# Exponentials on VectorE by the slot of four banks, layer-norm transposes by DMA, and two open sums in place of turn-taking by key chunk

## The chip, the cores and the metric

The kernel runs on one core of one Trainium2 chip. The metric is the device time of one execution in microseconds (us), the median of three runs. Engine names follow the profile: PE is the matrix engine (PEld its weight loads), DVE is VectorE, ACT is ScalarE, POOL is GpSimd, and SP is the engine whose queue (SPq) issues the DMAs.

## The reference, cut to what matters

One transformer layer over S = 2048 tokens of width D = 640, batch 1. The attention has 32 heads of 20 channels and no mask. The second half is a bilinear gate with 1728 hidden channels.

```python
x = A_x
h = x + attention(layernorm(x), A_wqkv, A_wo)       # softmax(q k^T / sqrt(20)) v, 32 heads
n = layernorm(h)
h2 = h + ((n @ B_w_gate) * (n @ B_w_up)) @ B_w_down
```

Inputs and output are bfloat16. The softmax needs 32 x 2048 x 2048 exponentials, and that is what the kernel is built around.

## The kernel before, in words

**Tiling.** Heads are taken in 8 groups of 4 (`G`, `HP`). The four heads of a group lie in the four 32-row bands of the partitions. Queries are cut into six blocks of 512, 512, 384, 256, 256 and 128 (`WIDTHS`). For a block `p` and a group `g`, scores are made transposed: 128 keys on the partitions, queries along the free side. A *slot* is (p, g, kg): 512 columns of (key tile, query) for each of the four heads, that is four PSUM banks of 128x512. There are 512 slots and 2048 banks. `att.flat` counts banks handed out.

**Exponentials.** PE fills one of two PSUM areas, `A0` of three banks and `A1` of two, with a burst of score matmuls (`s_act`), and ACT turns the area into a bf16 tile `E` with one ACTIVATE (`exp`, L731). The two areas alternate, so ACT instructions are of three banks and of two. About one bank in seven goes to DVE instead (`dexp`, `tail`, L738 to L790). DVE adds a bias and writes int16 (L745), and after every second bank it runs four more instructions over the pair (1024 columns: L769, L772, L775, L778), into tiles of their own (`i16`, `fr`, `hl`, `ED`). Such a bank comes from one of two spare PSUM banks `m` or from the third bank of `A0`. `SHARE` = 0.17 caps what DVE takes, counted from `D_START` = 128 banks.

**Sums.** For each slot PE multiplies E with V (`pv_act`) into one PSUM bank `acc`, which holds the four heads' 20 channels and their denominators. A *stretch* is a run of slots whose sum lies in `acc`. For the first block the first two groups take turns: four slots of group 0, four of group 1, then again for the next 512 keys, because the keys of chunk `c` of 512 come into being while the attention already runs. After each of the first three turns DVE copies or adds `acc` into an SBUF tile (`partial`, L873), and at the last turn `normalise` adds the rest (L898). `normalise` then sends the denominators out and back by three DMAs on SP's queue: `rs` (L905), a reciprocal on DVE (L906), `rd` (L907), `rb` (L911), and the product goes to `OnT` (L917).

**Projections.** Stage 1 (`stage1_ln`) makes the layer norm of four token tiles at a time on DVE and POOL. PE transposes each tile (five 128x128 blocks, `transpose_group`, L1009) and DVE or ACT copies the result into `lnT` (L1026, L1024). Keys and queries of groups 0 and 1 are projected straight into place (`proj_direct`). Those of groups 2 to 7 (`proj_dense`) are copied to `stg`, written to DRAM (`kq`, L1208, L1211), and read back spread out (`kT` L1225, `qT` L1222). Twenty small DMAs (L1237, L1243) put zeros into `kq`'s padding; each row that is read back needs them. V is projected in three parts (`proj_v`). The order and the due times of these groups stand at the end of the function (L1482 to L1520): V of a chunk is queued one chunk late, and `LEADK` = 16 brings the keys and queries of later groups forward.

**Second stage.** When a block's attention is done, `second_stage` (L1326) queues the output projection `wo`, the second layer norm (`l2`), its PE transposes into `ln2T` (L1376), the gate and up matmuls (`gs`, `hh`) and the down matmul (`ot`). For all blocks but the last ones this is background work that fills PE between score bursts.

**Order.** The function is a planner that runs while the program is built. It keeps a clock for each engine, and at each step it emits the instruction that its estimates put next (`Engines.run`, `Pe.choose`). What comes out is one fixed order for each engine and for SP's queue, and each engine works through its own strictly. Where the planner expects PE to be idle it puts in multiplications by zero (`fill`, tile `zt`).

Of the kernel before, what the change touches and what calls it, by code (L numbers as in the profile page):

```python
# [44 lines left out]
LASTP = len(WIDTHS) - 1  # L45
RES = 5
FAST_LAST = 2
# [145 lines left out]
class Pe:  # L193
# [91 lines left out]
    def fill(self, s):  # L285
        bank = self.att.summing()
        new = bank is None
        deps = [self.zeros]
        if new:
            b = next((b for b in self.mbanks if b.free.t is not None and b.free.t <= s), None)  # L290
            if b is None:
                b = Bank(self.att.acc)
                b.free = self.att.acc_free
            bank, deps = b.ap, deps + [b.free]
        n = bank.shape[1]
        self.charge(s, n / 2.4 + 3.0, self.shape(), float(n), deps, [])
        self.filler(bank, new)
# [30 lines left out]
NED = 4  # L328
NI16 = 3
# [10 lines left out]
LEADK = 16  # L340
# [4 lines left out]
def kernel(  # L345
# [26 lines left out]
    mb = tiles(psum, 2, [P, QW], F32, "m")  # L372
    pools = [tc.alloc_tile_pool(name="second", bufs=1, space=PSUM)]
    A = [None, pools[0].tile([P, 2, QW], F32, name="A1", tag="A1")]
    A[0] = pools[0].tile([P, 3, QW], F32, name="A0", tag="A0")

    def single_banks():

        if att.flat < att.total or att.a_free[0].t is None or att.a_free[1].t is None or len(pools) > 1:
            return  # L380
        pools[0].release()
# [18 lines left out]
    I16t = tiles(keep, NI16, [P, 2, QW], I16, "i16_")  # L400
    FR = tiles(keep, 2, [P, 2, QW], I16, "fr")
    HL = tiles(keep, 1, [P, 2, QW], BF16, "hl")
    ED = tiles(keep, NED, [P, 2, QW], I16, "ED")
    accS = tiles(keep, 2, [P, QW], F32, "accS")
    rb = tiles(keep, 2, [P, QW], F32, "rb")
    rs = tiles(keep, 6, [P, 16], F32, "rs")
# [64 lines left out]
    class Att:  # L471
        def __init__(self):
# [5 lines left out]
            for p, w in enumerate(WIDTHS):  # L478
                nb = NT * w // QW
                order = [[(g, kg) for kg in range(nb)] for g in range(G)]  # L480
                if p == 0:
                    order = [[(g, 4 * c + i) for i in range(4)] for c in range(NCH) for g in range(2)] + order[2:]
# [10 lines left out]
            self.sums = [len(r) for r in self.stretches]  # L493
# [10 lines left out]
            self.acc = acc[:]  # L504
            self.a_free = [Ev(0.0), Ev(0.0)]
            self.e_use = {0: [[] for _ in EA[0]], 1: [[] for _ in EA[1]], "ED": [[] for _ in ED]}
            self.e_n = {0: 0, 1: 0, "ED": 0}
# [4 lines left out]
            self.acc_free = Ev(0.0)  # L512
            self.dn = 0
            self.pair = []
            self.ipos = 0
            self.i_free = [Ev(0.0) for _ in I16t]
            self.f_free = [Ev(0.0) for _ in FR]
            self.h_free = [Ev(0.0) for _ in HL]
# [61 lines left out]
        def wants_d(self):  # L580
# [4 lines left out]
            if not self.pair and known([self.pv_ev[x] for x in self.e_use["ED"][self.e_n["ED"] % len(ED)]]) == INF:  # L585
                return False
            t = en.free["PE"]
            load = max(0.0, en.free["DVE"] - t) + sum(x.dur for x in en.pend["DVE"] if known(x.deps) < t + 400.0)
            return load < (D_LOAD if self.flat > 2 * HP * NT else D_LOAD0)
# [36 lines left out]
        def summing(self):  # L626

            if self.pv_at >= len(self.stretches):
                return None
            if self.pv_at in self.begun:  # L630
                return acc[:, 0:WIDTHS[self.slots[self.pv_left[0]][0]]]
            return None

        def between(self, t):
# [3 lines left out]
            return self.pv_at not in self.begun and self.acc_free.t is not None and self.acc_free.t <= t  # L638

        def s_option(self, t):  # L640
# [3 lines left out]
            if self.a_free[u].t is None:  # L644
                return INF, None, 0.0
            size = 3 - u
            banks = self.peek(size)
# [5 lines left out]
        def s_act(self, u, banks):  # L653
            def act(s):
                size = len(banks)
                deps = [self.a_free[u]]
# [56 lines left out]
                if self.flush or self.flat == self.total:  # L713
                    self.flush = False
                    if self.pair:
# [22 lines left out]
        def dexp(self, bank, b, ev, readers=None):  # L738
            k = self.ipos % len(I16t)
            pos = len(self.pair)  # L740
            self.taken += 1
            it = I16t[k]
# [4 lines left out]
            e = en.add("DVE", dve_ns(QW), [ev, self.i_free[k]], fn, 0)  # L747
            bank.free = e
            self.pair.append((b, e))
            if len(self.pair) == 2:  # L750
                self.tail()

        def tail(self):
            k = self.ipos % len(I16t)
            self.ipos += 1
            n = len(self.pair)
            N = n * QW
            it = I16t[k]
            fk, hk = self.dn % len(FR), self.dn % len(HL)
            self.dn += 1  # L760
            ek = self.e_n["ED"] % len(ED)
            self.e_n["ED"] += 1
            use = self.e_use["ED"][ek]
            self.e_use["ED"][ek] = sorted({b[0] for b, _ in self.pair})
            f, h, e16 = FR[fk], HL[hk], ED[ek]
            fb = f[:].bitcast(BF16)

            def p2():
                nc.vector.tensor_scalar(f[:, 0:n, :], it[:, 0:n, :], 127, None, ALU.bitwise_and)  # L769

            def p3():
                nc.vector.tensor_scalar(h[:, 0:n, :], f[:, 0:n, :], QR, QK, ALU.subtract, ALU.mult)  # L772

            def p4():
                nc.vector.tensor_tensor(fb[:, 0:n, :], h[:, 0:n, :], f[:, 0:n, :], ALU.mult)  # L775

            def p5():
                nc.vector.tensor_tensor(e16[:, 0:n, :], it[:, 0:n, :], fb[:, 0:n, :], ALU.add)  # L778

            e2 = en.add("DVE", dve_ns(N, 4), [e for _, e in self.pair] + [self.f_free[fk]], p2, 2)  # L780
            e3 = en.add("DVE", dve_ns(N, 4), [e2, self.h_free[hk]], p3, 2)
            e4 = en.add("DVE", dve_ns(N, 2), [e3], p4, 2)
            e5 = en.add("DVE", dve_ns(N, 2), [e4] + [self.pv_ev[s] for s in use], p5, 2)
            self.i_free[k] = e5
            self.f_free[fk] = e5
            self.h_free[hk] = e4
            eb = e16[:].bitcast(BF16)
            for i, (b, _) in enumerate(self.pair):
                self.E[b] = (eb[:, i, :], e5)
            self.pair = []  # L790

        def pv_option(self, t):
# [3 lines left out]
            for s in self.pv_left:  # L796
# [8 lines left out]
                if self.pv_at not in self.begun:  # L805
# [3 lines left out]
                    deps.append(self.acc_free)  # L809
                rt = max(t, known(deps))  # L810
                if rt < best[0]:
                    dur = sum(pe_ns(n) for _, _, n, _ in todo)
                    best = rt, self.pv_act(s, es, todo, deps, dur), dur, "C"
# [4 lines left out]
        def pv_act(self, s, es, todo, deps, dur):  # L818
            p, g, kg = self.slots[s]
            i_s = self.pv_at  # L820

            def act(start):
                pe.charge(start, dur, "C", dur * 2.4, deps, [self.pv_ev[s]])
                self.sums[i_s] -= 1
                first = i_s not in self.begun
                self.begun.add(i_s)
                last = self.sums[i_s] == 0
                for i, (k, q, n, c) in enumerate(todo):

                    opens = first and i == 0  # L830
                    ends = last and i == len(todo) - 1
                    for j in range(HP):
                        h = g * HP + j
                        mm(acc[32 * j:32 * j + 32, q:q + n], Vx[:, k, h * VS:h * VS + 32],
                           es[j][0][:, c:c + n], opens, ends)
# [3 lines left out]
                if last:  # L839
                    if p == 0 and g < 2 and kg < NCH * 3:  # L840
                        self.acc_free = partial(g, kg >= 4, self.pv_ev[s])
                    else:
                        self.acc_free = normalise(p, g, self.pv_ev[s])
# [27 lines left out]
    part_ev = {}  # L871

    def partial(g, more, ev):  # L873

        t = rb[g][:]
        if more:
            part_ev[g] = en.add("DVE", dve_ns(QW), [ev, part_ev[g]], lambda: nc.vector.tensor_tensor(t, acc[:], t, ALU.add), 0.3)
        else:
            part_ev[g] = en.add("DVE", dve_ns(QW), [ev], lambda: nc.vector.tensor_copy(t, acc[:]), 0.3)
        return part_ev[g]  # L880

    FAST = {LASTP: FAST_LAST, LASTP - 1: FAST_PREV}

    def normalise(p, g, ev):
# [11 lines left out]
        if p == 0 and g < 2:  # L896
            free = en.add("DVE", dve_ns(w), [ev, part_ev[g]] + was,
                          lambda: nc.vector.tensor_tensor(a[:, 0:w], acc[:, 0:w], rb[g][:], ALU.add), 0.5)  # L898
        else:
            free = en.add("DVE", dve_ns(w), [ev] + was,  # L900
                          lambda: nc.vector.tensor_copy(a[:, 0:w], acc[:, 0:w]), 0.5)
# [66 lines left out]

    rb_free = [Ev(0.0) for _ in range(8)]
# [60 lines left out]

    def sum_group(deps, mats, n, width, evac, tag):
# [53 lines left out]
    pe.zeros = e_zt  # L1085
    e_id = en.add("POOL", 1500.0, [], lambda: make_identity(nc, ident[:]), 0)
# [16 lines left out]
    def stage1_ln(ch):  # L1103
# [11 lines left out]
        for i in range(TPC):  # L1115
# [8 lines left out]
            def done(r, tt=tt, i=i, ev=ev):  # L1124
                lnT_ev[tt] = r
            g = transpose_group(outs[i], evs[i], lnT[:, :, tt * P:(tt + 1) * P], done,
# [199 lines left out]
    def second_stage(p):  # L1326
# [17 lines left out]
        for tt in range(nt):  # L1344
# [4 lines left out]
            for hf in range(2):  # L1349
# [9 lines left out]
                g = sum_group(T["wo_ev"] + [ex, Later(lambda: on_ev.get((p, G - 1)))], mats, HD, P, evac, f"W{p}{tt}{hf}")  # L1359
# [7 lines left out]
        for a in range(0, nt, step):  # L1367
# [4 lines left out]
            for i, e in zip(idx, evs):  # L1372
                def done(r, i=i):
                    lev[i].t2 = r
                lev[i] = Cell()
                g = transpose_group(l2[i % 2], e, ln2T[:, :, i * P:(i + 1) * P], done, "DVE", 1, f"t{p}{i}")  # L1376
                g.deps.append(fr.get("ln2T") or Ev(0.0))
                fr["ln", i % 2] = g.ev
                groups.append(g)
# [107 lines left out]

    def values(ch):
        for t in range(ch * TPC, (ch + 1) * TPC):
            g = proj_v(t, 0)  # L1490
            g.deps.append(first)
            pe.groups.append(g)

    for ch in range(1, NCH):
# [4 lines left out]
        values(ch - 1)  # L1499
    values(NCH - 1)  # L1500

# [5 lines left out]

    jobs = []
    for T_, when in enumerate((128, 192, 320, 384)):
        jobs.append((when - LEADK, len(jobs), proj_dense(0, T_, 0)))  # L1510
# [55 lines left out]
```

The softmax here doesn't subtract the row's maximum and nothing guards it: scores larger than these inputs give would overflow.

## Time and profile before

| what | us |
|---|---|
| median of 3 runs (lowest, highest) | 875.37 (875.25, 875.66) |
| the profiled execution | 875.66 |
| its span, first to last instruction | 873.6 |
| PE busy / ACT busy / DVE busy / POOL busy | 828.6 / 808.8 / 741.9 / 21.3 |
| first exponential starts | 17.02 |
| last exponential ends | 837.5 |

A busy time is the union of an engine's instructions, so two that overlap are not counted twice. "idle before" is how long the engine had nothing running ahead of an instruction, with the engine and line that ended the wait. A matmul's end is modelled, so a busy PE is not a PE at its peak.

### The profile page before, as it was taken

Reading aid. Unit: us, or ns where it says so; the run is one execution under the profiler, and the core shown is the slowest. Engines: PE = TensorE matmul, PEld = TensorE weight load, DVE = VectorE, ACT = ScalarE, POOL = GpSimd, SP = SyncE. Lnnn points to the kernel's source line nnn. Section 1 sums busy time; section 2 is a strip of 40 time slices with the busy share of each in tenths; the row PEclk is TensorE's granted clock in tenths of the full one; section 3 lists DMA queues with packets and bytes.
Section 4 is the critical chain, followed back from the end, with each engine's and each line's share of the span. In section 5 each row is a group of like instructions: output and inputs, shape, how many; then the busy total and the mean of one; then the engine's idle time right before and its main releaser. Section 6 shows DMA issues by size and latency. Waiting matters only on the chain.

```text
span 873.6 us, 35178 instructions
## 1 busy us (share of the span) xinstructions
PE 828.6 (95%) x15727; PEld 366.7 (42%) x15727; DVE 741.9 (85%) x1579; ACT 808.8 (93%) x771; POOL 21.3 (2%) x33
## 2 busy tenths in 40 slices
PE   6999999989999999999999999999999999999998
PEld 3344333223333322233444333344444444556676
DVE  5654587989879999999989999989999999889562
ACT  4789999999999999999999999999999999998931
POOL 3020000000000000000000000000000000000000
PEclk8899999999999999999999999999999999999999
DMA  7221221222221143320030223134024411164200
GB/s 209 64 58 49 79 67 31 78 76 67 69 79 29 28 105 103 78 63 18 30 91 13 57 66 81 27 84 105 17 51 94 96 32 32 32 150 86 52 6 24
DMA packets 131755, 56.23 MB, mean 64 GB/s; under 512 B 102292, under 2 KB 129556, under 8 KB 131604
## 3 DMA queue, kind: packets, MB, share of 16 engines
q1 hardware_dynamic: 131604, 53.99, 24.3%
q8 instruction: 123, 2.02, 1.0%
q14 instruction: 28, 0.23, 0.1%
HBM read 45.63 MB, written 8.09 MB: 61 GB/s over the span
## 4 chain that ended last, share of the span: by engine, by line
ACT 63%; PE 26%; DVE 6%; issue 5%; DMA 0%; DVEq 0%; POOL 0%; ACTq 0%
ACT E L731 62%; PE m L432 11%; PE A L432 6%; PE acc L432 5%; PE b L432 2%; DVE i L745 2%; DVE fr L775 1%; PE m L1017 1%; DVE ED L778 1%; DVE st L989 0%; DVE fr L769 0%; DVE hl L772 0%; DVE gs L1410 0%; DMA shared<-in_A_x_dram 0%; DVE shared L1001 0%
## 5 line engine op out<-in xcount | busy, mean ns | idle before, releaser
L731 ACT ACTIVATE E<-A 128x1536 bf16<-128x1536 f32 (+1 forms) x749 | 800.0, 1211 | 20.6 <-PE A L432 18.4
L432 PE MATMUL A<-qT,kT 32*128 32x256 bf16 (+3 forms) x3063 | 292.7, 298 | 24.1 <-ACT E L731 21.9
L432 PEld LDWEIGHTS <-kT 32*128 32x128 bf16 (+1 forms) x3448 | 100.1, 92 | 248.2 <-issue 215.0
L432 PE MATMUL acc<-E,Vx 128*32 128x256 bf16 (+3 forms) x2832 | 190.7, 304 | 4.8 <-ACT E L731 3.8
L745 DVE TENSOR_SCALAR i<-m 128x512 int16<-128x512 f32 x176 | 120.4, 685 | 13.5 <-PE m L432 12.5
L432 PEld LDWEIGHTS <-Vx 128*32 128x32 bf16 x3328 | 70.1, 95 | 100.5 <-issue 91.6
L775 DVE TENSOR_TENSOR fr<-hl,fr 128x1024 bf16<-128x1024 bf16 x151 | 103.4, 685 | 2.0
L778 DVE TENSOR_TENSOR ED<-i,fr 128x1024 int16<-128x1024 int16 x151 | 103.0, 682 | 1.3
L745 DVE TENSOR_SCALAR i<-A 128x512 int16<-128x512 f32 x126 | 86.5, 686 | 11.5 <-PE A L432 10.0
L432 PE MATMUL m<-Wd,hh 128*32 128x320 bf16 (+1 forms) x1498 | 79.9, 301 | 1.4 <-issue 0.9
L432 PE MATMUL m<-lnT,Wr 128*32 128x512 bf16 (+7 forms) x1200 | 74.7, 345 | 1.8 <-DVE lnT L1026 0.8
L432 PE MATMUL m<-ln2T,wu 128*32 128x512 bf16 (+2 forms) x980 | 69.5, 348 | 0.8 <-DVE i L745 0.4
L432 PE MATMUL m<-ln2T,wg 128*32 128x512 bf16 (+2 forms) x980 | 69.2, 349 | 0.3 <-DVE hh L1421 0.2
L432 PE MATMUL acc<-zt 128*32 128x512 bf16 (+3 forms) x1012 | 68.5, 346 | 0.0
L432 PE MATMUL m<-qT,kT 32*128 32x256 bf16 (+3 forms) x265 | 68.0, 310 | 0.0
L772 DVE TENSOR_SCALAR hl<-fr 128x1024 bf16<-128x1024 int16 x151 | 63.5, 421 | 1.5
L769 DVE TENSOR_SCALAR fr<-i 128x1024 int16<-128x1024 int16 x151 | 62.1, 417 | 0.7
L432 PEld LDWEIGHTS <-hh 128*32 128x32 bf16 (+2 forms) x1540 | 42.2, 96 | 28.1 <-issue 15.5
L1421 DVE TENSOR_TENSOR hh<-gs,m 128x512 bf16<-128x512 bf16 (+3 forms) x70 | 37.9, 541 | 14.0 <-PE m L432 10.1
L432 PE MATMUL m<-shared,On 128*32 128x320 bf16 x960 | 44.7, 300 | 0.7 <-DVE i L745 0.4
L432 PEld LDWEIGHTS <-Wr 128*32 128x32 bf16 (+1 forms) x1200 | 28.9, 97 | 27.0 <-issue 16.7
L1410 DVE CAST gs<-m 128x512 bf16<-128x512 f32 (+2 forms) x64 | 36.0, 562 | 4.7 <-PE m L432 4.3
(85 smaller groups left out, 542.7 us busy)
## 6 DMA issues: line engine op xcount, KB each, us to landing
wg<-in_B_w_gate_dram SPq DMA_DIRECT2D x47, 160.0 KB
wu<-in_B_w_up_dram SPq DMA_DIRECT2D x47, 160.0 KB
rb<-rd SPq DMA_DIRECT2D x16, 256.0 KB
kT<-kq SPq DMA_DIRECT2D x24, 128.0 KB
kq<-stg SPq DMA_DIRECT2D x24, 120.0 KB
out_dram<-ot SPq DMA_DIRECT2D x16, 160.0 KB
shared<-in_A_x_dram SPq DMA_DIRECT2D x14, 160.0 KB
Wd<-in_B_w_down_dram SPq DMA_DIRECT2D x13, 160.0 KB
```

The source lines that it names most:

```text
L432: nc.tensor.matmul(out_, lhsT=lhsT, rhs=rhs, start=start, stop=stop)
L731: apart(readers, nc.scalar.activation(E[:, 0:size, :], src[:, 0:size, :], ACT.Exp, scale=LN2_ / UNIT))
L745: apart(readers, nc.vector.tensor_scalar(it[:, pos, :], bank.ap, BIAS, 0.0, ALU.add, ALU.max))
L769: nc.vector.tensor_scalar(f[:, 0:n, :], it[:, 0:n, :], 127, None, ALU.bitwise_and)
L772: nc.vector.tensor_scalar(h[:, 0:n, :], f[:, 0:n, :], QR, QK, ALU.subtract, ALU.mult)
L775: nc.vector.tensor_tensor(fb[:, 0:n, :], h[:, 0:n, :], f[:, 0:n, :], ALU.mult)
L778: nc.vector.tensor_tensor(e16[:, 0:n, :], it[:, 0:n, :], fb[:, 0:n, :], ALU.add)
L1017: nc.tensor.transpose(pt[32 * i:32 * i + 32, c * P:(c + 1) * P], src[:, c * P + 32 * i:c * P + 32 * i + 32], ident[:])
L1410: r = en.add("DVE", dve_ns(w), [e, was], lambda: nc.vector.tensor_copy(gs[0:M, 0:w], ps[0:M, 0:w]), 1)
L1421: r = en.add("DVE", dve_ns(w), [e, ce, was], lambda: nc.vector.tensor_tensor(hh[0:M, 0:w], gs[0:M, 0:w], ps[0:M, 0:w], ALU.mult), 1)
```

## The change

Four things change, and since the planner works from estimates, the order on every engine moves with them.

1. **DVE's exponentials.** The pairs become groups of a whole slot. Four banks go to one int16 tile `D` (three such tiles), and the four following instructions then run over 2048 columns at once, the last one in place. `ED`, `i16` and the second `fr` go. `D_START` falls from 128 to 96 and the limit `D_LOAD0` goes.
2. **Transposes.** Those of token chunks 2 and 3 in stage 1, and all of the second stage, become `dma_start_transpose` on SP's queue (`turn_rows`). Chunks 0 and 1 stay on PE.
3. **The first two groups.** Their slots of block 0 form one stretch. Group 1 sums in a second bank `acc2`, so `partial` goes. The bank is taken from `A0`, which has two banks instead of three until both sums are closed.
4. **The order of projections.** V is queued in its own chunk, and V, keys and queries of later groups are queued by simple loops without `LEADK`.

A path `last_quotients` is added for `TURNED` groups; `TURNED` is 0, so nothing of it runs but two small memsets of its tiles `o7`. Its code is left out below, as is bookkeeping of `acc_free` as a pair.

```diff
-NED = 4
-NI16 = 3
+ND = 3
-LEADK = 16
+TURNED = 0
+TURN = 2
-    A[0] = pools[0].tile([P, 3, QW], F32, name="A0", tag="A0")
+    early = tc.alloc_tile_pool(name="early", bufs=1, space=PSUM)
+    A[0] = early.tile([P, 2, QW], F32, name="A0", tag="A0")
+    acc2 = early.tile([P, QW], F32, name="acc2", tag="acc2")
+    late = []
...
-                    order = [[(g, 4 * c + i) for i in range(4)] for c in range(NCH) for g in range(2)] + order[2:]
+                    order = [[(g, 4 * c + i) for c in range(NCH) for g in range(2) for i in range(4)]] + order[2:]
...
+        def acc_of(self, p, g):
+            return acc2[:] if (p, g) == (0, 1) else acc[:]
...
             size = 3 - u
+            if u == 0 and not late and (self.acc_free[1].t is None or self.pv_at == 0 or self.acc_free[1].t > at):
+                size = 2
...
+                if size == 3 and not late:
+                    early.release()
+                    late.append(tc.alloc_tile_pool(name="late", bufs=1, space=PSUM))
+                    A[0] = late[0].tile([P, 3, QW], F32, name="A0", tag="A0")
...
         def dexp(self, bank, b, ev, readers=None):
...
-            e = en.add("DVE", dve_ns(QW), [ev, self.i_free[k]], fn, 0)
+            e = en.add("DVE", dve_ns(QW), [ev] + self.duse, fn, 0)
             bank.free = e
-            self.pair.append((b, e))
-            if len(self.pair) == 2:
-                self.tail()
+            self.group.append((b, e))
 
         def tail(self):
...
+            n = len(self.group)
             N = n * QW
...
-                nc.vector.tensor_tensor(e16[:, 0:n, :], it[:, 0:n, :], fb[:, 0:n, :], ALU.add)
+                nc.vector.tensor_tensor(it[:, 0:n, :], it[:, 0:n, :], fb[:, 0:n, :], ALU.add)
...
-    def partial(g, more, ev):
-
-        t = rb[g][:]
-        if more:
-            part_ev[g] = en.add("DVE", dve_ns(QW), [ev, part_ev[g]], lambda: nc.vector.tensor_tensor(t, acc[:], t, ALU.add), 0.3)
-        else:
-            part_ev[g] = en.add("DVE", dve_ns(QW), [ev], lambda: nc.vector.tensor_copy(t, acc[:]), 0.3)
-        return part_ev[g]
...
+    def turn_rows(src, dst, deps, prio):
+
+        return dma(lambda: nc.sync.dma_start_transpose(dst, src), deps, prio=prio, size=2 * P * D * 2)
...
+            if ch >= TURN:
+                lnT_ev[tt] = turn_rows(outs[i], lnT[:, :, tt * P:(tt + 1) * P], [evs[i]], 0)
+                ln_free[i] = lnT_ev[tt]
+                continue
...
-                lev[i] = Cell()
-                g = transpose_group(l2[i % 2], e, ln2T[:, :, i * P:(i + 1) * P], done, "DVE", 1, f"t{p}{i}")
-                g.deps.append(fr.get("ln2T") or Ev(0.0))
-                fr["ln", i % 2] = g.ev
-                groups.append(g)
+                lev[i] = turn_rows(l2[i % 2][:], ln2T[:, :, i * P:(i + 1) * P], [e, fr.get("ln2T")], 0.5)
+                fr["ln", i % 2] = lev[i]
...
         pe.groups += [proj_direct(1, 0, ch), proj_direct(1, 1, ch)]
-        values(ch - 1)
-    values(NCH - 1)
+        pe.groups += [proj_v(t, 0) for t in range(ch * TPC, (ch + 1) * TPC)]
...
-    jobs = []
+    vq = [(t, 1) for t in range(NT)] + [(t, 2) for t in range(NT)]
     for T_, when in enumerate((128, 192, 320, 384)):
-        jobs.append((when - LEADK, len(jobs), proj_dense(0, T_, 0)))
+        due([proj_dense(0, T_, 0)], when)
         for ch in range(NCH):
-            jobs.append((when + 16 * ch - LEADK, len(jobs), proj_dense(1, T_, ch)))
-    for part, when in ((1, 128), (2, 256)):
-        for t in range(NT):
-            jobs.append((when + 4 * t, len(jobs), proj_v(t, part)))
-    for when, _, g in sorted(jobs, key=lambda x: x[:2]):
-        due([g], when)
+            due([proj_dense(1, T_, ch)], when + 16 * ch)
+            due([proj_v(*vq.pop(0)) for _ in range(4) if vq], when + 16 * ch + 16)
...
-D_START = 2 * HP * NT
+D_START = 96
-D_LOAD0 = 600.0
```

## Prediction

> **What bounds the kernel now.** I read the page's busy times and chain first, then ACT's instructions by shape.
>
> ```profile
> PE 828.6 (95%) x15727; PEld 366.7 (42%) x15727; DVE 741.9 (85%) x1579; ACT 808.8 (93%) x771; POOL 21.3 (2%) x33
> ...
> ACT 63%; PE 26%; DVE 6%; issue 5%; DMA 0%; DVEq 0%; POOL 0%; ACTq 0%
> ```
>
> ```profile
> L731 ACT ACTIVATE E<-A 128x1024 bf16<-128x1024 f32 x501 | 500.2, 1072 | 9.7 <-PE A L432 8.7 <-PE acc L432 0.6
> ...
> L731 ACT ACTIVATE E<-A 128x1536 bf16<-128x1536 f32 x248 | 370.1, 1492 | 10.9 <-PE A L432 9.7 <-ACT E L731 0.4
> ```
>
> ACT carries 63% of the chain that ended last, nearly all in L731. The mean durations overlap, so I price by the median distance from one start to the next: 0.904 us for two banks, 1.330 for three. The 749 take 501 x 0.904 + 248 x 1.330 = 782.7 us of the 820.5 between first start (17.0) and last end (837.5). PE's 95% holds some 77 us of zero filling. The missing 38 us are gaps, the long ones early; ACT's timeline has them in brackets:
>
> ```profile
> 35.04 5.97 ACT L731 ACTIVATE E<-A 128x1536 bf16<-128x1536 f32 x5 [2.86 <-PE A L432]
> ...
> 55.16 29.75 ACT L731 ACTIVATE E<-A 128x1024 bf16<-128x1024 f32 x26 [3.52 <-PE A L432]
> 86.17 27.04 ACT L731 ACTIVATE E<-A 128x1024 bf16<-128x1024 f32 x24 [1.26 <-PE A L432]
> ```
>
> The first two are the waits for chunk 1's and chunk 2's keys; 86.17 is where head group 2 begins. SP's timeline shows how group 2's queries came in time: their read (L1222) goes out before the denominators of groups 0 and 1 (L905).
>
> ```profile
> 32.09 0.48 SPq L1237 DMA_DIRECT2D kq<-zt  x1
> 56.18 1.95 SPq L1269 DMA_DIRECT2D shared<-in_A_wo_dram  x3
> ...
> 76.17 0.44 SPq L1222 DMA_DIRECT2D qT<-kq  x1
> ...
> 79.79 0.60 SPq L905 DMA_DIRECT2D rs<-accS  x1
> ...
> 86.23 0.56 SPq L905 DMA_DIRECT2D rs<-accS  x1
> ```
>
> The hole from 32.6 to 56.2 shows that SP's queue is strict: L1269 waits for POOL, and all stand behind it. At the end PE binds: the last block's transposed norm is ready at 849.7, but PE comes to use it at 857.3.
>
> ```profile
> 848.55 0.45 PE L1014 MATMUL b<-ident,l 128*128 128x128 bf16 x5 [0.32 <-DVE l L1001]
> ...
> 857.27 1.29 PE L432 MATMUL b<-ln2T,qT 128*128 128x128 bf16 x20
> ```
>
> [...] The trace has 0.22 us for a block on PE and no DMA transpose at all.
>
> **The change, part by part.** Counts and order are those of the two built programs, which can be read without running them.
>
> *Exponentials.* DVE takes 317 banks instead of 302. ACT runs 528 twos and 225 threes: 477.3 + 299.3 = 776.6 us, **-6.2 us**. ACT is at its limit, so this is on the path.
>
> *DVE.* Four rows tell the price of a pair.
>
> ```profile
> L775 DVE TENSOR_TENSOR fr<-hl,fr 128x1024 bf16<-128x1024 bf16 x151 | 103.4, 685 | 2.0
> L778 DVE TENSOR_TENSOR ED<-i,fr 128x1024 int16<-128x1024 int16 x151 | 103.0, 682 | 1.3
> ...
> L772 DVE TENSOR_SCALAR hl<-fr 128x1024 bf16<-128x1024 int16 x151 | 63.5, 421 | 1.5
> L769 DVE TENSOR_SCALAR fr<-i 128x1024 int16<-128x1024 int16 x151 | 62.1, 417 | 0.7
> ```
>
> A pair costs 2.21 us, 151 of them 333 us. [...] Fifteen more first passes add 10, 24 copies fewer of transposed blocks save 12, `partial` saves 4: DVE falls by some 35 us. From 280 to 720 us it is busy 424.7 of 440. Yet relief shortens nothing by itself, as ACT ends last there. I take 1 us off later gaps (bounds 0 and 6). Against it, a 1.22 us instruction ahead of a first pass holds a bank up to 0.54 us longer than one of 0.68; the third bank of `A0`, used 120 times, has about 1 us to spare, so I take nothing (bounds 0 and 3).
>
> *PE transposes away, filling added.* 24 tiles leave PE; the fillings rise from 274 to 331 quads. Both lie beside ACT. After the last burst PE has 30.3 us of work by columns instead of 29.9: **+0.5 us**.
>
> *The two open sums.* `A0` has two banks for the first 128 banks: 64 ACT instructions where there were 51. Already in the sum.
>
> *DMA transposes.* A tile is 160 KB. Bounds: 1.8 us from issue to landing (`out<-ot`, the same size, by the trace's semaphore events)[...]. I take about 3 us, overlapping, so chunk 2's four tiles, normalised by about 43.6 (44.8 in this trace, less `partial` and some of chunk 3's statistics queued ahead), lie in `lnT` by 48 to 51. On SP they pass the zero padding and the output-weight loads. DVE's writes of chunk 3's norms wait for them, and V and key copies are queued behind these on DVE. At the very end the transpose may take 8 us before PE misses it.
>
> *Where the order leaves ACT idle.* PE's order between two bursts gives a least gap. I price four matmuls side by side from the lines with many in a row: 0.22 us at 512 columns (36 in 2.13 us), 0.08 at 160 (40 in 0.93), 0.15 at 320 between them.
> - Chunk 1: a run of 2.1 us where there were 3.6; gap 1.0, and 0.4 at a small one later.
> - Chunk 2 (burst 32): after the exponentials that it waits for, PE has queued V, one projection, the keys and 0.9 us of filling: 4.5 us, so a gap of 5.1 with 0.6 for the hand-overs, from about 49 to 54, if the transposes are there by 51.
> - **Group 2 (burst 64).** After the last sum of group 1, which needs the exponentials of burst 63, PE has queued one sum (0.2), three V tiles of 160 (1.2), three projections (3.3), five V tiles of 320 (3.75) and eleven fillings (2.4): 10.1 by columns alone, 10.9 at my prices. SP forces a wait too: the queries' read now stands behind `rd` of group 1, which needs that sum, its copy, `rs` and the reciprocal. That chain is 1.3 us (sum and copy, 84.9 to 86.2 in this trace) + 1.9 (`rs` landing) + 0.3 + issues of 0.4, 0.75 and 0.35 + 3.0 (`qT<-kq` landing) = 8.0. So even without the filling the gap would be about 8. I take 10.8.
> - A run of 2.8 us at burst 103: 1.0.
>
> With the 0.7 at 25.3 as it is, early gaps are 0.7 + 1.0 + 0.4 + 5.1 + 10.8 + 1.0 = 19.0. Before they were 0.69 + 2.86 + 1.05 + 3.52 + 1.26 + 1.17 = 10.6. **+8.4 us.**
>
> **Sum:** -6.2 + 8.4 - 1.0 + 0.5 = +1.7. The profiled execution took 875.7 (span 873.6 and 2.1 around it), 0.3 over the median of 875.4. So 877.1.
>
> **The rivals.**
> - *A, the forecast:* the exponentials saved are given back at group 2's start. 877.1; with the bounds of relief and chunk 2, 874 to 881. Chance 0.5.
> - *B, the transposes by DMA are slow.* Nothing in this trace excludes it. From some 2 us a tile in series, chunk 2's keys come late. At 4 us: 42.6 + 16 + about 2.5 for projection and copy = 61 against 54, +7, and chunk 3, whose norms wait for the same buffers, adds 1.5: 885.6. [...] Chance 0.22.
> - *C, faster: DVE's load was what kept ACT from its rhythm.* The place is 115 to 790 us. Beside the gaps, ACT's small delays (each under 0.3 us beyond the median distance) sum to 16 us in the run, and DVE frees the banks that bursts wait for. If the relief returns 40% of these 16, that is 6 us: 871. It decides from 3.5 us returned. Against it: waits of PE's bursts for DVE are put at 0.6 us in total. Chance 0.28.
>
> **How the numbers follow.** About 0.2% (1.75 us) is what can be told from no change, so 873.6 to 877.1 is "same". Slower holds B and rather more than half of A: 0.53. Same holds the rest of A and a little of C: 0.24. Faster holds the rest of C: 0.23. The range 870.5 to 887.5 takes in C's and B's centres[...]. A's own range stands above.
>
> **What would show it.** Right: ACT idle by 8 to 11 us once, after 64 two-bank exponentials, with `qT<-kq` issued after `rd`; 753 ACT instructions at unchanged distances; PE still last at the end. Wrong: that gap under 4 us (the order says otherwise), a gap well over 5 us before burst 32 (B), or ACT's distances from 115 to 790 nearer the medians (C). DVE's instructions over 2048 columns should show 0.69 and 1.22 us.

## The result and the profile after

The changed kernel takes 890.35 us (median of 4 runs, 888.42 to 891.75), the kernel before in runs beside it 875.31. The ratio is 1.017, 95% interval 1.015 to 1.019: slower by 15 us, above the range of the forecast. The profiled execution has a span of 888.2 us and took 890.3.

The page after, engines and chain:

```profile
PE 837.5 (94%) x15481; PEld 367.3 (41%) x15481; DVE 723.8 (81%) x1280; ACT 803.3 (90%) x775; POOL 22.9 (3%) x35
...
ACT 59%; PE 27%; DVE 7%; issue 5%; DMA 1%; SPq 0%; DVEq 0%; POOL 0%; ACTq 0%
```

ACT and DVE have less to do than before (808.8 and 741.9), and yet the span is longer: the time went into waiting. The exponentials by shape (instructions, then busy us and mean ns, then idle time before them and what ended it):

```profile
L748 ACT ACTIVATE E<-A 128x1024 bf16<-128x1024 f32 x528 | 523.7, 1065 | 18.8 <-PE A L438 15.8 <-PE acc L438 1.3 <-PE m L438 0.6
L748 ACT ACTIVATE E<-A 128x1536 bf16<-128x1536 f32 x225 | 336.5, 1496 | 21.5 <-PE m L438 16.0 <-PE A L438 5.2
```

Counts as forecast; the distance from start to start is still 0.904 us for two banks and 1.330 for three (medians in the trace). The idle time has doubled, from 20.6 to 40.3 us, and 16.0 of it is one wait. ACT's timeline, idle time in brackets:

```profile
33.95 11.11 ACT L748 ACTIVATE E<-A 128x1024 bf16<-128x1024 f32 x12 [1.41 <-PE A L438]
45.76 1.94 ACT L748 ACTIVATE E<-A 128x1024 bf16<-128x1024 f32 x2 [0.71 <-PE A L438]
48.24 1.94 ACT L748 ACTIVATE E<-A 128x1024 bf16<-128x1024 f32 x2 [0.54 <-PE A L438]
56.79 29.73 ACT L748 ACTIVATE E<-A 128x1024 bf16<-128x1024 f32 x32 [6.62 <-PE A L438]
102.52 28.01 ACT L748 ACTIVATE E<-A 128x1536 bf16<-128x1536 f32 x26 [16.00 <-PE m L438]
```

Group 2 starts at 102.5 instead of 86.2. A table by banks of exponentials finished says where the rest lies; it joins the count of banks in the built program to ACT's start times in the trace (us; the start column ends when group 2 starts, at bank 128):

| kernel | start | banks 128 to 1792 | 1792 to 2040 | from 2040 to the end | span |
|---|---|---|---|---|---|
| before | 86.2 | 641.7 | 105.6 | 40.1 | 873.6 |
| after | 102.5 | 634.9 | 110.9 | 39.9 | 888.2 |
| difference | +16.3 | -6.8 | +5.3 | -0.2 | +14.6 |

The saving of some 6 us on ACT is there, in the long middle. It is overrun by the start (+16.3), and a smaller loss stands near the end (+5.3).

A burst is the score matmuls for one ACTIVATE; bursts are counted from 0, so burst 64 is group 2's first. What stood there? SP's timeline after, the transposes of stage 1 first:

```profile
41.69 5.31 SPq L1056 DMA_TRANSPOSE lnT<-shared  x4
...
51.18 4.69 SPq L1056 DMA_TRANSPOSE lnT<-shared  x3
...
90.21 0.52 SPq L912 DMA_DIRECT2D rb<-rd  x1
90.79 0.69 SPq L1277 DMA_DIRECT2D kq<-zt  x1
91.57 0.53 SPq L908 DMA_DIRECT2D rd<-rr  x1
...
93.56 0.38 SPq L1256 DMA_DIRECT2D qT<-kq  x1
```

The same two steps before (the write of zeros is L1243 there; the read of the queries is the row at 76.17 in the prediction):

```profile
73.99 0.67 SPq L1243 DMA_DIRECT2D kq<-zt  x1
```

In both kernels the read of group 2's queries goes out 2 to 3 us after the last of the twelve writes of zeros into the query buffer. In the planner these writes form a chain, each waiting for the one before, and the read needs the last. That one goes out at 74.0 before and at 90.8 after. On the chip it is a matter of order alone: in the changed kernel the last write landed at 97.5, 3.9 us after the read had gone out.

PE and VectorE inside the long wait, after:

```profile
93.78 1.41 PE L438 MATMUL m<-Wr,lnT 128*32 128x320 bf16 x36
98.14 0.62 PE L438 MATMUL m<-zt 128*32 128x512 bf16 x4 [2.95 <-DVE Vx L1288]
98.52 2.37 PE L438 MATMUL m<-lnT,Wr 128*32 128x512 bf16 x20
...
102.03 0.39 PE L438 MATMUL A<-qT,kT 32*128 32x512 bf16 x3
```

```profile
96.99 0.69 DVE L918 TENSOR_TENSOR On<-accS,rb 128x512 bf16<-128x512 f32 x1 [3.06 <-DMA rb<-rd]
97.60 0.89 DVE L1288 CAST Vx<-m 128x320 bf16<-128x320 f32 x2
```

By my estimate from the durations in the trace before, PE's queue alone would have taken 10.9 us. But VectorE stands at a quotient (L918) that waits for its broadcast `rb`, issued at 90.21 and landed at 96.97; the copies of values are queued behind it, and PE, with two buffers `m`, waits for these copies: 2.95 us of idle time.

A second thing in that wait is no part of the change. The run e2 below has PE's order of the changed kernel up to burst 64 and also waits 2.98 us for the copies. Yet its twenty matmuls after that take 1.26 us where the changed kernel's take 2.37, and its wait is 14.7 us:

```profile
97.23 1.26 PE L438 MATMUL m<-lnT,Wr 128*32 128x512 bf16 x20
```

The view by windows has the clock that PE was granted as the third number from the end, first for the changed kernel, then for e2:

```profile
98.00:101.00 3.00, 2.86 (x28) 1.21 (x31) 0.55 (x3) 0.00 (x0) 0.00 (x0) 0.51 0.45 106
```

```profile
97.00:99.60 2.60, 2.58 (x52) 1.50 (x51) 1.22 (x3) 0.00 (x0) 0.00 (x0) 1.00 0.43 117
```

So about 1.3 us of the 16.0 (the difference to e2's 14.7) belong to a clock of half speed in this one execution.

### The profile page after: what moved, and what is told of

It reads as the page before. It is cut to its first block, busy times and chain, and to the rows that moved or that the text cites. A ratio compares the mean times of both kernels' runs of the same rounds, so it can differ in the third digit from the quotient of the medians.

```text
span 888.2 us, 34459 instructions
## 1 busy us (share of the span) xinstructions
PE 837.5 (94%) x15481; PEld 367.3 (41%) x15481; DVE 723.8 (81%) x1280; ACT 803.3 (90%) x775; POOL 22.9 (3%) x35
## 4 chain that ended last, share of the span: by engine, by line
ACT 59%; PE 27%; DVE 7%; issue 5%; DMA 1%; SPq 0%; DVEq 0%; POOL 0%; ACTq 0%
ACT E L748 59%; PE m L438 12%; PE A L438 7%; PE acc L438 5%; PE b L438 3%; DVE D L766 2%; DMA rb<-rd 1%; DVE fr L787 1%; DVE fr L781 1%; DVE hl L784 1%; DVE st L1012 0%; DVE accS L902 0%; DVE D L790 0%; PE m L1040 0%; DVE Vx L1288 0%
## 5 line engine op out<-in xcount | busy, mean ns | idle before, releaser
L748 ACT ACTIVATE E<-A 128x1536 bf16<-128x1536 f32 (+1 forms) x753 | 794.5, 1194 | 40.3 <-PE A L438 21.0
L766 DVE TENSOR_SCALAR D<-m 128x512 int16<-128x512 f32 x197 | 134.2, 684 | 26.1 <-PE m L438 24.8
L787 DVE TENSOR_TENSOR fr<-hl,fr 128x2048 bf16<-128x2048 bf16 (+1 forms) x80 | 96.3, 1203 | 0.7
L790 DVE TENSOR_TENSOR D<-D,fr 128x2048 int16<-128x2048 int16 (+1 forms) x80 | 96.2, 1203 | 0.3
L766 DVE TENSOR_SCALAR D<-A 128x512 int16<-128x512 f32 x120 | 82.1, 684 | 13.7 <-PE A L438 12.2
L438 PE MATMUL acc<-zt 128*32 128x512 bf16 (+3 forms) x1192 | 85.0, 348 | 0.0
L438 PE MATMUL m<-qT,kT 32*128 32x256 bf16 (+3 forms) x289 | 76.1, 314 | 0.0
L781 DVE TENSOR_SCALAR fr<-D 128x2048 int16<-128x2048 int16 (+1 forms) x80 | 54.5, 681 | 1.0
L784 DVE TENSOR_SCALAR hl<-fr 128x2048 bf16<-128x2048 int16 (+1 forms) x80 | 54.4, 680 | 1.0
L438 PEld LDWEIGHTS <-hh 128*32 128x32 bf16 (+2 forms) x1540 | 42.4, 96 | 27.8 <-issue 16.8
L438 PEld LDWEIGHTS <-zt 128*32 128x32 bf16 x1324 | 32.7, 97 | 35.5 <-issue 24.3
```

Source lines behind the costliest of these rows:

```text
L438: nc.tensor.matmul(out_, lhsT=lhsT, rhs=rhs, start=start, stop=stop)
L748: apart(readers, nc.scalar.activation(E[:, 0:size, :], src[:, 0:size, :], ACT.Exp, scale=LN2_ / UNIT))
L766: apart(readers, nc.vector.tensor_scalar(it[:, pos, :], bank.ap, BIAS, 0.0, ALU.add, ALU.max))
L781: nc.vector.tensor_scalar(FR[:, 0:n, :], it[:, 0:n, :], 127, None, ALU.bitwise_and)
L784: nc.vector.tensor_scalar(HL[:, 0:n, :], FR[:, 0:n, :], QR, QK, ALU.subtract, ALU.mult)
L787: nc.vector.tensor_tensor(fb[:, 0:n, :], HL[:, 0:n, :], FR[:, 0:n, :], ALU.mult)
```

## The experiments

The expectations name their theories by letters. G: the order that the planner writes is the loss. J: the job order alone is. P: the padding chain. Q: DMA is too slow in itself. V: long VectorE instructions. S: the second-stage transposes. W: the quotient's wait. In e1, e3 and e6 the planner put the last block's DMA transpose ahead of some matmuls of the gate projection of the block before. These matmuls read the next block's norms, so a part of the computation is changed there, and PE stands 2.7 us for the transpose near the end. Later versions let the transpose wait for that projection ("gate wait"):

```diff
-                ups.append(gu.ev)
+                ups.append(Max([gg.ev, gu.ev]))
```

**e1, stage 1 by matmul.**

```diff
-TURN = 2
+TURN = 4
```

> Chunks 2 and 3 of stage 1 are transposed by matmul again, all else as in the changed kernel. Theory G (the long idle stretch of ScalarE at the start of head group 2 comes from the stage-1 transposes by DMA: they make the projections late in the planner's reckoning, and the planner then puts them in one run between two bursts): PE's runs ahead of bursts 16, 32, 64, 88 and 93 are now 2.1, 4.0, 2.1, 3.5 and 4.3 us by columns, where the changed kernel has 5.9 at 32, 11.0 at 64 and 2.8 at 103; a gap of 1 to 3 us after each, 10 to 12 us in sum instead of 28, so 873 to 876 us. Rival J (the gap comes from the new order of the projection jobs, or from the two open sums): a gap of 10 us or more stays at burst 64, and the time stays at 885 to 890.

Measured: 881.0 us, ratio 1.007 (1.004 to 1.009). The wait at burst 64 is gone:

```profile
84.33 5.76 ACT L748 ACTIVATE E<-A 128x1024 bf16<-128x1024 f32 x5 [1.87 <-PE A L438]
```

Job order and open sums were the changed kernel's, so J falls. The time is 5 us above what G expected. Of this 2.7 is a stall after the last exponential, which nobody had foreseen:

```profile
851.79 0.58 PE L438 MATMUL b<-ln2T,kT 128*64 128x256 bf16 x2 [2.74 <-DMA ln2T<-l]
```

**e12, the same with the gate wait.**

> The changed kernel with the stage-1 transposes by matmul, as in the first experiment, but with the transposes into ln2T waiting for the last gate projection too. In the first experiment the last block's transpose was put ahead of two of that projection's matmuls: PE stood 2.7 us for it, and these two matmuls read the next block's norms. Theory: 881.0 - 2.7 = 878.3 us, the rest unchanged. Rival (the wait merely moves to the next matmul): 881.

Measured: 877.6 us, ratio 1.004 (1.002 to 1.005). That is 3.4 us under e1, and 2.4 by the ratios, whose intervals overlap; 2.7 was expected. In the trace PE no longer stands for `ln2T`.

**e2, second stage by matmul.** The lines of `second_stage` that call `turn_rows` are put back to `transpose_group`.

> The second stage's norms are transposed by matmul again, all else as in the changed kernel. Theory S (the transposes by DMA in the second stage cost time late in the kernel, by holding SP's queue ahead of the weight loads): the gaps of ScalarE after 790 us fall from 9 to about 5, 886 us. Theory V (the late gaps come from the longer VectorE instructions, or from work that the early gap pushed to the end): late gaps stay near 9, 889 to 891. The gap of 16 us at burst 64 stays in both.

Measured: 889.5 us, ratio 1.018 (1.015 to 1.021), no different from the changed kernel. The wait at burst 64 is 14.9 (beyond the median distance; 16.1 in the changed kernel by that measure). From bank 1792 on it takes 107.7 + 45.5 = 153.2 us, where the changed kernel takes 110.9 + 39.9 = 150.8. The late stretch did shrink by 3 us, as S had it, but what comes after bank 2040 grew by more. As a price in sum S falls.

**e3, the job order of before.** The `jobs` list sorted by due time, with `LEADK = 16`, is put back.

> The projection jobs are sorted and given their lead of 16 banks as in the kernel before, all else as in the changed kernel. Rival J: the gap at burst 64 goes, about 876 us. Theory G: it stays, since PE's run ahead of burst 64 is 12.7 us by columns (11.0 in the changed kernel): a gap of 13 to 18 us, 888 to 893 us.

Measured: 899.8 us, ratio 1.028 (1.025 to 1.032). The wait at burst 64 grows to 22.0 us by the same measure, longer even than G expected; part of it is a granted clock of half speed from 97.0 to 103.9 (0.8 to 0.9 in the page's slice from 89.6 to 112.0). The old order alone repairs nothing.

**e4, pairs instead of slots.**

```diff
             self.group.append((b, e))
+            if len(self.group) == 2:
+                self.tail()
```

> VectorE's exponentials are finished in pairs of banks again (instructions over 1024 columns, seven smaller buffers for three large), all else as in the changed kernel. Theory V: late gaps fall from 9 to about 5 us, 886 us. If batching only relieves VectorE, which is off the path: VectorE's busy time rises by some 29 us and the time stays at 889 to 892. If the relief is worth something on the path (the 1 us of the prediction, or up to 6): 891 to 896.

Measured: 892.3 us, ratio 1.020 (1.018 to 1.022), which overlaps the interval of the changed kernel. The time doesn't decide: it is just above the 889 to 892 of a relief that is off the path, and within the 891 to 896 of one that is on it. The trace says more. DVE is busy for 763.4 us, 40 more, and ACT's small delays (each up to 0.3 us beyond the median distance) sum to 15.3 us, against 15.5 in the changed kernel and 15.9 before. So VectorE's relief returned nothing where it was looked for, in ACT's small delays; that it is worth a us or two elsewhere isn't excluded.

**e5, padding that doesn't wait for padding** (with the gate wait). `PADP` is 0.5 where the priority was 1.5, and a lower number goes out earlier. So two things change at once: the chain goes, and the writes move forward.

```diff
-            e_pad0 = dma(pad, [e_zt, e_pad0], size=8 * 12 * QW * 2, prio=1.5)
+            pads.append(dma(pad, [e_zt], size=8 * 12 * QW * 2, prio=PADP))
+    e_pad0 = Max(pads)
```

> The twelve writes of zeros that fill the padding of the query buffer (L1277) no longer wait for one another; all else, the transposes by DMA too, as in the changed kernel, except that the transposes into ln2T also wait for the last gate projection. Theory P (the queries of group 2 can't be read before the last of these writes, and the transposes by DMA push this chain back on SP's queue): PE's run of 11.0 us ahead of burst 64 goes from the order, and the gap of 16.1 us falls below 4; chunk 2's gap rises with its run (6.8 us instead of 5.9), and PE has 2.0 us more to do after the last burst: 890.4 - 13 + 1 + 2 = 880 us (877 to 883). Rival Q (SP's queue or the DMA engines are too slow for the queries whatever the order): a gap over 10 us stays at burst 64, 888 or more.

Measured: 880.1 us, ratio 1.005 (1.003 to 1.006). All stage-1 transposes by DMA are still there, and the wait at burst 64 is 1.7 us. ACT, e5:

```profile
57.71 29.60 ACT L749 ACTIVATE E<-A 128x1024 bf16<-128x1024 f32 x32 [8.94 <-PE A L439]
89.02 30.09 ACT L749 ACTIVATE E<-A 128x1536 bf16<-128x1536 f32 x28 [1.71 <-PE A L439]
```

All twelve writes are out by 30.6, ahead of the first transpose, and the query read goes out at 56.9 instead of 93.6. Q falls. P holds for the place of the writes; what their chain and what their priority did to it is not told apart. Chunk 2's wait grew to 8.9, and banks 1792 to 2040 take 114.3 us.

**e6, the quotients later.**

```diff
             deps.append(Later(lambda: wo_done.get(p - 1)))
+        elif g < 2:
+            deps.append(att.s_ev[0, 2])
```

> The quotients of groups 0 and 1 (L918) are put behind the copies of values in VectorE's order; up to burst 64 nothing else differs from the changed kernel, PE's order included. Only the gap at burst 64 is to be read, since the order after it differs (a run of 5.7 us at burst 104). Theory W (3 us of the 16 come from the value copies that stood behind a quotient that waited for its broadcast): the gap falls from 16.1 to about 13, where the landing of the queries then sets it. Rival: PE's work and its waits for its two buffers make the gap alone: it stays at 15.5 to 16.5.

Measured: 901.8 us in one execution, with the longer run at burst 104 in it. Read at burst 64 alone, e6:

```profile
104.39 3.71 ACT L748 ACTIVATE E<-A 128x1536 bf16<-128x1536 f32 x3 [13.60 <-PE m L438]
```

16.0 became 13.6. But PE's granted clock is 1.00 here, so the fair comparison is with e2's 14.7: some 1.1 us came from values queued behind a waiting quotient. W holds in kind, for less than the 3 us expected; the comparison is of single executions. PE's stretch from the end of group 1's sum to burst 64 is now 12.7 us, 1.8 of it idle: 10.9 of work, as priced. The rest hangs on the landings. `rb`, issued at 94.49, landed at 101.31, and five transfers issued behind it between 95.1 and 97.9, the queries last, landed in order from 101.8 to 103.3.

**e7, slot batches in the kernel before.** `dexp` and `tail` of the changed kernel, with its buffers, are put into the kernel before.

> The kernel before with one part of the change: VectorE's exponentials in batches of a whole slot. ScalarE has 520 instructions of two banks and 232 of three, 778.6 us instead of 782.7 (-4.1). The early order of PE is unchanged; a run of 6.2 us at burst 556 makes a gap of 5 where the kernel before has gaps of 2.4 and 1.0 at bursts 406 and 546. If batching only relieves VectorE: 875.3 - 4.1 + 2 to 4 = 873 to 875. If VectorE's relief also takes delays from ScalarE's rhythm (rival C of the prediction): 867 to 870. If long instructions hold up PE late (theory V): 877 to 880.

Measured: 881.7 us, ratio 1.007 (1.005 to 1.009), slower than the theory of pure relief gave. Banks 1792 to 2040 take 104.7 us, less than before, so the loss isn't the late one. The largest piece is the run that had been seen in PE's order:

```profile
631.77 1.02 ACT L725 ACTIVATE E<-A 128x1024 bf16<-128x1024 f32 x1 [5.41 <-PE acc L430]
```

**e8, second-stage transposes in the kernel before** (with the gate wait).

> The kernel before with another part alone: the second stage's norms transposed by DMA (with the wait for the last gate projection as well). ScalarE 781.0 us instead of 782.7 (-1.7); PE's work after the last burst 33.1 us instead of 29.9 (+3.2). If the transposes are hidden: 876 to 878. If they hold up the last blocks (theory S): late gaps grow from 4.6 to 9, 881 to 883.

Measured: 874.4 us, ratio 0.999 (0.999 to 1.000). They are hidden, and worth nothing.

**e11, both of these in the kernel before.**

> The kernel before with its own early order, its turn-taking sums and its stage 1, and with the two parts that stand outside these: batches of a whole slot and second-stage transposes by DMA (with the wait for the last gate projection). Batches alone cost 6.5 us, of which 5.5 lay in one run of PE that this order hasn't got (its longest are 3.8 at 25 and 4.2 at 718); the transposes alone cost nothing. ScalarE 778.4 us (-4.3), PE's work after the last burst 29.8. Theory G: 875.2 - 4.3 + 0 to 3 = 871 to 874 us. Theory V: 876 to 880.

Measured: 873.6 us, ratio 1.000 (0.999 to 1.001). The run that cost e7 its 5 us isn't in this order, and the loss is gone with it: V falls as an explanation of e7. But banks 1792 to 2040 take 113.2 us, after a run of 4.2 us at burst 718.

**e9, changed kernel with stage 1 by matmul, job order of before and gate wait; e10, the same with no transpose by DMA at all.**

> The changed kernel with the stage-1 transposes by matmul and with the job order of the kernel before, together (each alone was slower than the kernel before); the transposes into ln2T also wait for the last gate projection. Batches of a slot, the two open sums and the transposes by DMA in the second stage stay. PE's runs between bursts: 2.1 us at 16, 4.0 at 32, 2.8 at 64, none above 2.6 after: early gaps of about 1.5 + 0.8 + 3 + 2 = 7.5 us instead of 28. ScalarE 777 us, PE 28.9 us of work after the last burst (30.3 in the changed kernel). Theory G (the loss is the order that the planner writes, not the price of any added operation): 17.3 + 777 + 7.5 + 9 to 12 of later and small gaps + 15 of small delays + 35 to 37 after = 863 to 869 of span, 865 to 871 us. Rival V (four-bank batches, or two open sums, cost PE or ScalarE time by themselves late in the kernel, some 5 us more): 874 to 880.

> The same, and the second stage's norms by matmul as well: no transpose by DMA at all. One run of PE of 5.2 us at burst 580 (a gap of 4), PE's work after the last burst 29.8 us (+0.9). Theory G: 867 to 873 us, 2 to 4 above the run beside it. If the second-stage transposes by DMA cost anything by themselves: below the run beside it.

Measured: e9 871.0 us, ratio 0.997 (0.996 to 0.998); e10 869.4 us, ratio 0.995 (0.994 to 0.997). Both beat the kernel before. e9 is just at the edge of what G gave. e10 was expected 2 to 4 us above e9 and came out 1.6 below. The intervals overlap, but a small price of the second-stage transposes in this order, of a us or two, isn't excluded. e9 differs from e12 by the job order alone, and that is worth 6.6 us here.

**e13, every part of the change, with free padding, the job order of before and the gate wait.**

> Every part of the change stays, the stage-1 transposes by DMA too; the padding writes don't wait for one another, the job order is that of the kernel before, and the transposes into ln2T wait for the last gate projection as well. PE's runs: 2.1 us at burst 16, 6.5 at 32, 2.9 at 64, 4.5 at 724; ScalarE 777.0 us; PE 28.7 us of work after the last burst. If the order was the whole loss: gaps 0.5 + 1.5 + 8.7 + 2.5 early, 5 in the middle, 6 late, 15 of small delays, 34.5 after the end: 17.3 + 777 + 39 + 34.5 = 868 of span, 869 to 872 us; the 9 us at chunk 2 is then the price of the stage-1 transposes, some 5 more than with transposes by matmul, and the rest is as in the fastest runs. If they also cost time elsewhere (DMA engines, SP's queue): 876 to 880.

Measured: 870.0 us, ratio 0.994 (0.992 to 0.996): 5.6 us under the kernel before, and 20 under the changed kernel, with all its operations. It differs from e5 by the job order alone, which is worth 10 us here. SP and ACT, e13:

```profile
25.61 4.67 SPq L1279 DMA_DIRECT2D kq<-zt  x7
...
41.67 5.30 SPq L1058 DMA_TRANSPOSE lnT<-shared  x4
...
56.93 0.54 SPq L1258 DMA_DIRECT2D qT<-kq  x1
```

```profile
56.69 29.60 ACT L750 ACTIVATE E<-A 128x1024 bf16<-128x1024 f32 x32 [7.69 <-PE A L440]
89.31 21.48 ACT L750 ACTIVATE E<-A 128x1536 bf16<-128x1536 f32 x19 [3.03 <-DVE Vx L1291]
```

The query padding is out before the first transpose, and group 2 starts with a wait of 3 us. Chunk 2 still waits 7.7 us, where e9, with transposes by matmul, has 2.7 between the same two bursts. The table for those that matter (us):

| kernel | start | banks 128 to 1792 | 1792 to 2040 | from 2040 to the end | span |
|---|---|---|---|---|---|
| e12, stage 1 by matmul | 85.1 | 638.9 | 107.6 | 41.2 | 872.8 |
| e5, free padding | 89.0 | 633.1 | 114.3 | 42.4 | 878.8 |
| e9 | 85.2 | 636.7 | 107.0 | 39.6 | 868.5 |
| e10 | 84.7 | 638.3 | 104.4 | 40.0 | 867.4 |
| e11 | 84.0 | 635.1 | 113.2 | 39.4 | 871.7 |
| e13 | 89.3 | 631.3 | 107.8 | 38.9 | 867.3 |

## Why the prediction was wrong, step by step

- *Exponentials, -6.2:* right. 528 and 225 instructions at 0.904 and 1.330 us; the middle of the run is 6.8 us shorter.
- *DVE:* the prices over 2048 columns, which no trace of before showed, were right, and the relief was worth nothing. VectorE's instructions over 2048 columns, after:

```profile
L787 DVE TENSOR_TENSOR fr<-hl,fr 128x2048 bf16<-128x2048 bf16 x77 | 93.4, 1214 | 0.7
...
L781 DVE TENSOR_SCALAR fr<-D 128x2048 int16<-128x2048 int16 x77 | 52.8, 686 | 0.9
```

1.214 and 0.686 us, within 1% of what was expected. The summed durations on VectorE fell by 37 us (forecast 35), the busy time, in which overlaps count once, by 18. The 1.0 us that I took off was not there: small delays went from 15.9 to 15.5, and pairs (e4) have 15.3. Rival C had its mechanism wrong.
- *PE's tail, +0.5:* right in kind; the stretch after the last exponential is 36.2 us after and 36.1 before.
- *DMA transposes, about 3 us:* right, as an estimate: the trace before showed only its lower bound, 1.8 us for a plain transfer of the size. Alone one lands 2.6 us after its issue, and four in a row landed at 44.4, 45.8, 47.1 and 48.4, at the early edge of 48 to 51. Rival B falls as it was put: chunk 2's transposes were in time. Against `out<-ot`, a plain transfer of the size, it lands 0.5 us later (2.6 against a median of 2.1 after), and its issue is longer: each takes SP 1.2 to 1.5 us as a rule, where that plain transfer takes 0.34.
- *Chunk 1 and chunk 2:* 1.0 + 0.4 and 5.1 were forecast; the brackets show 1.41 + 0.71 + 0.54 and 6.62. The runs of PE were right, the waits for its two buffers missing; in chunk 2's run PE stands twice for a copy of values, 0.43 us each.
- *Group 2, 10.8 us:* this step failed in its size (16.0); place and sign were right. I added up PE's queue by columns (10.9 at my prices, which e6 confirms) and SP's chain separately (8.0), and took the larger. Neither sum held the broadcast `rb`, which took 6.8 us to land. The quotient that waits for it holds the value copies, and these hold PE's buffers: 2.95 us. The half-speed clock of this execution is some 1.3 us more. The last us or so, with the hand-overs between engines that I had counted at chunk 2 and not here, isn't taken apart. The queries landed 5.4 us after their issue instead of the 3.0 that I took, behind `rb` in the same queue. That was at 99.0, 3 us before PE came to use them, so they weren't what the burst waited for last.
- *The reason behind it:* I named the place of the query read on SP, behind `rd`, but not what had put it there. I had written that the transposes "pass the zero padding" and had not asked who waits for the padding. In the planner the read needs the last of twelve chained writes. e5 frees these writes and moves them forward, keeps the transposes, and the wait is gone; e1 takes the stage-1 transposes away, and the wait is gone too.
- *The end, +5.3, was not in the sum at all.* I priced PE's work after the last burst, and not PE's runs between the late bursts. It is not settled which step of the change brings it: it is smaller without second-stage transposes (e2: 107.7 us for banks 1792 to 2040, with a longer end), smaller with pairs (e4: 148.4 from bank 1792 on), and there in e11 (113.2) although e7 and e8, with one part each, have 104.7 and 104.5. The old job order took it from 114.3 (e5) to 107.8 (e13). It goes with where the planner leaves runs of PE, that much is argued; no run shows what would fix it in the changed kernel alone.

In sum: +16.3 at the start where I had +8.4, +5.3 late where I had nothing, no relief. Is the loss a price of the operations? In the main no: e13 has all of them and is faster than the kernel before. It was the order in which they were issued. One price may be left: e13 starts group 2 at 89.3, e9 with matmul transposes in stage 1 at 85.2, and most of the difference is chunk 2's wait. Whether that is the transfers themselves or PE's order around them, no run shows.

The job order, which e3 clears of the wait at burst 64, isn't harmless. Putting the old one back cost 9 us in the changed kernel (e3; 2.7 of them are PE's stall for `ln2T`), but saved 6.6 where stage 1 was by matmul (e12 to e9) and 10 where the padding was free (e5 to e13). One and the same edit had either sign, depending on the order around it.

## What to carry to other kernels

When a step moves to a queue that serves in order (SP's stood from 32.6 to 56.2 us behind one wait in the trace before), list what it passes and follow each passed item to its last reader: twelve small writes of zeros, idle filler before, came to decide when a head group could start. Where a planner writes the order, judge a change by the order it gives (the runs of one engine between two deadlines), and try the neighbouring orders before giving up the change: the same operations took from 870 (e13) to 900 us (e3). Two waits on one engine's path don't just give the larger of two sums, if the items of one stand in the other's queue: here the sums were 10.9 and 8.0, and the wait was 16.0 us, 1.3 of them by the clock. And before a wait in one trace is taken apart, see what clock the engine was granted in it (0.51 and 1.00 for the same matmuls here).

## What the runs showed of the hardware

A transpose by DMA of 128x640 bf16 from SBUF to SBUF holds SP for 1.2 to 1.5 us as a rule (2.1 to 2.2 in three of the 24), over three times as long as a plain transfer of the size (0.34), and four in a row landed 1.3 us apart. A broadcast of 256 KB (`rb`) landed 6.8 us after its issue here (median 5.1), and the five smaller transfers (8 to 128 KB) issued within 4 us behind it all landed after it, in order, within 2 us. In e6 it was the same (6.8, and then five within 2 us). So here a transfer's time to land went with what was ahead of it in the queue: for the queries 5.4 us, and 2.5 in e5, with no broadcast ahead. PE's granted clock fell to half for 3.4 us in the changed kernel's trace (97.5 to 101.0; 0.51 in the view from 98 to 101) and did not in e2's (1.00 from 97.0 to 99.6), with the same order and the same idle time before: twenty matmuls of 512 columns took 2.37 us and 1.26.
